# A gated mix of a spectral filter and a long convolution on one Trainium2 core: weight rows copied by ScalarE, a third butterfly on TensorE, half-width gated matrices, and a new instruction order

## The chip, the cores and the metric

The kernel runs on one core of one Trainium2 chip. The metric is the device time of one execution in microseconds (us), as the median of several executions; the span is the part of it from the first to the last instruction that the profiler recorded. A core has these engines, each with a queue of its own that it works through in order: PE (TensorE, matrix products; PEld is its loading of weights), DVE (VectorE), ACT (ScalarE), POOL (GpSimd) and SP (SyncE, which here only issues DMAs). They wait for one another by semaphores. DMAs run on 16 DMA engines, whichever queue issued them.

## What is computed

The reference, cut to what matters (x is 2048 time steps by 512 channels; the tensor u is not used):

```python
g = sigmoid((x * gate_w).sum(-1, keepdims=True))          # one gate per time step

X = rfft2(x, axes=(time, channel))                        # branch a: spectral filter
a = irfft2(X * (w_r + 1j * w_i))

dt = exp(log_dt)                                          # branch b: long convolution
A = -exp(log_A_real) + 1j * A_imag
C = (C_real + 1j * C_imag) * dt[:, None]
K = 2 * einsum("dn,dnl->dl", C, exp(A * dt[:, None] * pos)).real
b = irfft(rfft(x, 2 * L) * rfft(K, 2 * L))[:L] + x * D_skip

out = g * a + (1 - g) * b
```

The step sizes in the inputs are so small that every K is constant over the 2048 steps, so the convolution is a running sum of x times one factor per channel. The kernel counts the channels for which this holds and has a general path for the case that one is missing; that path does not run with these inputs.

## The kernel before

All tensors are float32. Branch a is a two-dimensional Fourier transform written as matrix products. Time, 2048, is split into 32 x 64, channels are folded into four groups of 128 (`CHANNELS`), and the spectrum is worked off in eight *units* (0 to 7), each with two of 16 frequency slots. Branch b and the gate run beside it on the same engines.

The order of the work is written out by hand in `PLAN` (lines 29 to 38): a list of words, a letter for a step and a number for its index. A dictionary maps each letter to a function (lines 623 to 630), and the words are emitted in that order. Since every engine works in order, the list fixes the order on every queue; the tile framework adds the semaphores. The steps, with their engines:

- `F` (POOL, L254 to 260) folds one of the ten parts of x, `C` (PE, L263) is the first time stage of a part, `c` (DVE, L276) transposes its result into `AR`. x is loaded into `AI`, whose space is later used for the spectrum of the last stages.
- `P` (PE, L429) is the second time stage of a unit with matrices `s2e`, `t` (ACT, L434) copies it to `et`, `D` (PE, L447) is the channel transform with `dfw`, into the tile `p_d`. `d` (ACT, L456) copies half of `p_d` to `ds`, and `Z` (DVE, L464 to 472) is the butterfly of even and odd channel parts. For the units in `ZPE` the butterfly is done on PE instead, by 16 more instructions in `D` (L451 with `zfw`), and `d` and `Z` are absent.
- `W` and `U` (DVE, L484) multiply by the weights `w` of the unit, `p` (POOL, L490 and 491) combines real and imaginary parts, `g` (POOL, L503 and 504) is the butterfly of the way back, `h` (ACT, L511 to 519) repairs partition 0, where a special frequency lies.
- `I` (PE, L531) is the inverse channel transform, `i` (ACT, L537) copies half of it, `V` (DVE, L545) writes sums and differences into `AI`.
- `K` (PE and ACT, L551 and 553) repairs slot 0. `B` (PE, L565, eight of them) is the first inverse time stage and needs all units; before the first one (`FIRSTB`) stand `NDUM` dummy matmuls (L559). `b` (DVE, L569) transposes.
- `Q` (PE, L588, eight of them) is the last stage. Its matrices `s1a` have been multiplied by the gate before: `S` loads one of four, `E` (DVE, L582) multiplies both its halves by the gate. `q` (DVE, L602) adds branch b and issues the output DMA; for `LASTQ` it goes in two halves (L599).
- Branch b: `X` loads x transposed, 1 MB for each of four channel groups, into `XT`; `x` (ACT, L336) copies one half into a PSUM tile, `m` (DVE, L339) scans, `y` (ACT, L348) scales the scan into `v`, `o` (ACT, L343) scales x by the skip factors, `r` (POOL queue, L353) is a DMA that adds `v` into `XT`, `H` (POOL, L371) multiplies by the gate's complement.
- The gate: `k` (PE, L376) is one group of four matmuls over `XT`, `G1` (ACT, L386) the sigmoids, `G2` (SP) writes the gate to memory, `O` (SP, L363) reads it back as a broadcast into `gb`, `u` (ACT, L367) copies it to a PSUM tile for `E`. `N` and `G4`, `G5` belong to the count.
- Loads: `l` (SP, L415) loads a unit's weights of 512 KB; there are four such buffers, which the four `s1a` use afterwards. `R` and `T` (SP) load constants and parameters.

Row 0 of each unit's weight tile is replaced by a special row (the weights of one more channel frequency). `J` (L399 to 410) prepares these rows: three tiny DVE operations, ACT copies, a transpose on PE with the unit matrix `eye`, and a copy to `hT`. `L` (SP, L418) then copies 2 KB of `hT` into the tile by a DMA, which must wait until the unit's own `w` has landed.

Units 1 and 7, the first ones, are cut into halves: 11 and 21 are the two halves of unit 1, 17 and 27 those of unit 7.

PSUM tiles (two banks each) come from one pool of four (`psum`, L186): `C`, `P`, `D`, `I`, `x`, the gate sums, `u`, `K`, `B` and `Q` each take the next of the four in the order of the list and wait until the tile's last reader has finished. The 13 buffers `blk`, which hold `f`, `et`, `tw`, `px` and `gt`, go round in the same way, and so do four buffers `v` for `y` and `O`.

Of the kernel before, what the change touches and what calls it, by code (L numbers as in the profile page):

```python
# [29 lines left out]
F2 X1 C0 R7 C1 c0 R6 J0 c1 F3 J1 R9 C2 c2 F4 C3 c3 F5 R1 R0 C4 J2 F6 C5 c4 C6 c5 F7 F9 T0 F8 c6 C7 c7 C8 C9 c8 c9 P17  # L30
P27 l7 x1 P11 X0 N1 t17 t27 D17 D27 d17 P21 m1 N3 L7 l1 N0 N4 d27 N2 y1 Z17 l4 t11 Z27 l6 P4 t21 P6 L1 U17 W17 X2 x0
U27 W27 L4 t4 m0 D11 d11 k0 D21 k1 k2 p17 t6 D4 X3 y0 Z11 d21 l5 k3 R10 D6 U11 W11 p27 g17 g27 h27 o3 R4 p11 o2 h17 L6
Z21 R8 L5 U21 d4 W21 Z4 U4 o1 P5 G1 R5 I17 I27 W4 d6 Z6 W6 P0 l0 U6 i17 t5 g11 p21 g21 o0 i27 h21 G2 r1 V27 V17 x2 D5
l2 m2 p4 g4 O2 h4 L0 l3 t0 D0 h11 I11 y2 d0 O0 U5 P2 o5 o4 t2 W5 I4 S1 p6 Z0 i11 U0 L3 L2 r0 W0 I21 g6 h6 V11 i4 i21
S0 D2 p5 g5 V4 h5 V21 d2 Z2 r2 W2 U2 P3 x3 t3 D3 p0 g0 S2 h0 m3 y3 U3 u0 W3 E1 I6 p2 o7 i6 o6 E0 V6 I5 I0 i5 V5 g2 h2
I2 G4 O3 i0 V0 p3 g3 h3 S3 I3 i2 G5 V2 u1 E3 K0 i3 H2 K1 V3 E2 B1 b1 O1 r3 B5 b5 H4 B0 b0 H0 H3 B2 b2 B3 b3 B4 H1 b4
H6 B7 b7 B6 Q0 Q2 q0 H5 Q3 H7 b6 q2 q3 Q5 Q1 q5 q1 Q7 q7 Q6 q6 Q4 q4
# [3 lines left out]
_T = np.arange(128)  # L41
# [6 lines left out]
def _consts():  # L48

    pi = np.pi  # L50
    a = np.arange(32)
    b = np.arange(64)
    k2 = np.arange(64)
    b_ = b.reshape(2, 32)
    S1 = np.zeros((32, 2, 32))
    S1[:, 0, 0] = 1
    S1[:, 1, 0] = (-1.0) ** a
    for s in range(1, 32):
        f = s if s < 16 else s - 16 + 0.5
# [53 lines left out]
    s2q = np.stack([s2p[0], s2p[1] @ inv, s2p[2] @ inv], 1)  # L113
# [3 lines left out]
    c, s = np.cos(th), np.sin(th)  # L117
# [22 lines left out]
    for x in range(2):  # L140
# [38 lines left out]
def body(ctx: ExitStack, tc: tile.TileContext, x, xg, xt, w, wh, prms, vecs, gw,  # L179
         c_s1e, c_s1f, c_s2e, c_s2, c_s2v, c_s2r, c_s2q, c_s1b, c_s1a, c_dfw, c_zfw, c_dbw, c_pos, c_eye, out):  # L180
# [5 lines left out]
    def psum(name):  # L186
        return ps.tile([P, 2, 512], F32, tag="ps", name=name)
# [33 lines left out]
    hT = work.tile([32, P], F32, name="hT")  # L221
    gws = work.tile([P, 4, 32], F32, name="gws")
# [7 lines left out]
    t_ = {}  # L230

    with tc.manual_schedule():
        prm = {}
        ldt = few[:, 0]
        nc.scalar.dma_start(s1e, c_s1e)
        nc.scalar.dma_start(hw, wh)
        nc.scalar.dma_start(eye, c_eye)
# [62 lines left out]
        def n1():  # L300
            S.activation(few[:, 0], few[:, 0], AF.Exp)
# [109 lines left out]

# [5 lines left out]
        def load_h(u):  # L417
            nc.sync.dma_start(t_["w", u][0:1, 0], hT[4 * u:4 * u + 4])  # L418
# [155 lines left out]
        def load_a(k):  # L574
            s1a[k] = work.tile([P, 8, P], F32, tag="w", name="s1a", bufs=4)
            nc.sync.dma_start(s1a[k], c_s1a[k])

        def gated(k, E):
            s = s1a[k].rearrange("p b (e c) -> p b e c", e=2)
            g = (t_["gp", k // 2] if E is V else t_["gb", 2 + k // 2]).rearrange("p (b c) -> p b c", c=64)[:, 8 * (k % 2):8 * (k % 2) + 8]  # L580
            for e in range(2):
                E.tensor_tensor(s[:, :, e], s[:, :, e], g, op=ALU.mult)  # L582

        def Q_(j):
            i, k = j // 4, j % 4
            p = t_["pq", j] = psum("p_oa").rearrange("p u (b c) -> p (u b) c", b=4)
            for b in range(8):
                T.matmul(p[:, b], VA[:, i, 8 * (k % 2) + b, :, k // 2], s1a[k][:, b], start=True, stop=True)  # L588
# [16 lines left out]
        def a_a(j):  # L605
# [11 lines left out]
            lambda: (nc.sync.dma_start(gws, gw), nc.sync.dma_start(dsk, vecs[:, 1])),  # L617
            lambda: (nc.sync.dma_start(s2v, c_s2v), nc.sync.dma_start(s2r, c_s2r)),
# [17 lines left out]
    with tc.If(n_small < D):  # L636
        with tc.tile_pool(name="dram", bufs=1, space=bass.MemoryType.DRAM) as dp:
            Kd = dp.tile([D, L], F32, name="Kd")
            with tc.tile_pool(name="kg", bufs=1) as kg:

                pos = kg.tile([P, 96], F32, name="pos")
                nc.sync.dma_start(pos, c_pos)
                ld = kg.tile([P, 4], F32, name="ld")
# [141 lines left out]
            for k in range(4):  # L785
                nc.sync.dma_start(ga[k], c_s1a[k])
# [33 lines left out]
def _arrays(given):  # L820
# [12 lines left out]
    w = np.stack([w[:, :, :, 0, 0], w[:, :, :, 1, 1], w[:, :, :, 0, 1], w[:, :, :, 1, 0]], 3)  # L833
    arrays = {
# [39 lines left out]
```

## Time and profile before

| | |
|---|---|
| median of 3 runs | 119.42 us (119.1 to 120.74) |
| the profiled execution's own time | 119.98 us |
| its span | 118.1 us |
| mean granted TensorE clock | 0.969 of full speed |
| PE busy | 96.8 us (82% of the span) |
| DVE busy | 88.0 us (74%) |
| POOL busy | 75.1 us (64%) |
| ACT busy | 45.6 us (39%) |
| DMA | 28.79 MB, mean 244 GB/s |

How to read the profile. A row of a group of instructions gives line, engine, operation, the tiles written and read, shapes and count; then busy time in us and the mean duration of one in ns; then the idle time of the engine just before these instructions and what ended it. The chain of work is followed back from the last instruction to what released each step; its rows give the start, the length and what it was. A stage row gives a window and its length, then busy time (and count of instructions) of PE, PEld, DVE, ACT and POOL, the granted TensorE clock, the share of time that the DMA engines were busy, and GB/s. A row of waits gives the waiting engine and line, what it waited for, the total in us, how many times, and the longest. SPq is the DMA issuing of SP. Durations of operations that follow one another closely overlap a little, so that two of 1.28 us can start 1.23 us apart.

### The profile page before, as it was taken

The page shows a single profiled execution, that of the slowest core. Times are in us where ns is not written, and L with a number is a line of the kernel's source. Part 1 is how long each engine was busy: PE and PEld are TensorE (multiplying, and loading weights), DVE is VectorE, ACT ScalarE, POOL GpSimd, SP SyncE. Part 2 cuts the span into 40 slices and gives each one's busy share as a digit, 9 for nine tenths or more (in the row PEclk, how much of TensorE's full clock was granted, in tenths as well). Part 3 has the DMA queues.
Part 4 walks back from the last instruction along what each step waited for, and adds up shares of the span by engine and source line. Part 5 has one row for each costly group of instructions (what it writes and reads, how often), then busy time and mean ns, then how long its engine had stood idle before and what let it go on. Part 6 is the DMA issues. An engine that isn't in the chain of part 4 may idle for free.

```text
span 118.1 us, 2316 instructions
## 1 busy us (share of the span) xinstructions
PE 96.8 (82%) x877; PEld 78.7 (67%) x877; DVE 88.0 (74%) x139; ACT 45.6 (39%) x80; POOL 75.1 (64%) x70
## 2 busy tenths in 40 slices
PE   6989784999861999968495978997899999999700
PEld 6957463999430649967395977987753359999700
DVE  0059889848988439999649599999798999956620
ACT  0320004359549059391878283698740000000000
POOL 0069580220796005999999999999999999910000
PEclk9999999999999679999999999999999999999985
DMA  3999999977979976499979999978129700678680
GB/s 66 381 389 416 413 383 345 298 318 238 327 286 337 409 226 220 136 325 178 225 191 214 262 321 218 262 198 297 50 44 190 126 3 3 248 314 330 248 302 15
DMA packets 9314, 28.79 MB, mean 244 GB/s; under 512 B 1577, under 2 KB 2121, under 8 KB 8781
## 3 DMA queue, kind: packets, MB, share of 16 engines
q1 hardware_dynamic: 7628, 23.93, 55.9%
q0 software_dynamic: 1088, 4.19, 19.5%
q10 hardware_dynamic: 576, 0.43, 1.1%
q8 instruction: 9, 0.15, 0.5%
q14 instruction: 13, 0.10, 0.3%
HBM read 20.12 MB, written 4.21 MB: 206 GB/s over the span
## 4 chain that ended last, share of the span: by engine, by line
PE 46%; DMA 29%; POOL 10%; DVE 3%; ACT 3%; issue 2%; SPq 1%; DVEq 0%; POOLq 0%
PE p_oa L588 13%; PE p_d L447 10%; DMA s2e<-in_c_s2e_dram 8%; PE p_ia L565 6%; DMA XT<-in_xt_dram 6%; PE p_t L429 6%; PE p_v L531 6%; DMA AI<-in_x_dram 6%; POOL gt L504 4%; DMA s1a<-in_c_s1a_dram 4%; DMA w<-in_w_dram 3%; DMA last<-in_c_s1e_dram 3%; POOL gt L503 2%; POOL px L490 2%; PE p_gate L376 2%
## 5 line engine op out<-in xcount | busy, mean ns | idle before, releaser
L447 PE MATMUL p_d<-et,dfw 128*128 128x256 f32 (+1 forms) x80 | 18.7, 370 | 4.2 <-ACT et L434 3.2
L484 DVE TENSOR_TENSOR tw<-p_d,w 128x1024 f32<-128x1024 f32 (+1 forms) x20 | 19.2, 1005 | 1.2 <-ACT ds L456 0.6
L371 POOL TENSOR_TENSOR XT<-XT,gb 128x1024 f32<-128x1024 f32 x8 | 19.2, 2755 | 0.0
L447 PEld LDWEIGHTS p_d<-et,dfw 128*128 128x128 f32 x80 | 12.9, 202 | 8.4 <-ACT et L434 4.7
L531 PE MATMUL p_v<-dbw,gt 128*128 128x128 f32 x128 | 15.8, 278 | 2.5 <-POOL px L490 1.2
L429 PE MATMUL p_t<-s2e,AR 128*128 128x128 f32 x128 | 16.2, 282 | 1.6 <-DMA s2e<-in_c_s2e_dram 1.6
L429 PEld LDWEIGHTS p_t<-s2e,AR 128*128 128x128 f32 x128 | 15.8, 196 | 2.0 <-DVE AR L283 1.8
L531 PEld LDWEIGHTS p_v<-dbw,gt 128*128 128x128 f32 x128 | 14.9, 192 | 3.2 <-ACT gt L512 1.4
L283 DVE STREAM_TRANSPOSE AR<-p_s 128x512 f32<-128x512 f32 (+1 forms) x20 | 10.7, 587 | 7.3 <-PE p_s L275 7.3
L503 POOL TENSOR_TENSOR gt<-px 128x512 f32<-128x512 f32 (+1 forms) x10 | 11.0, 1101 | 7.8 <-PE p_d L447 7.3
L588 PEld LDWEIGHTS p_oa<-s1a,AR 128*128 128x128 f32 x128 | 15.2, 196 | 0.8 <-DVE AR L569 0.8
L588 PE MATMUL p_oa<-s1a,AR 128*128 128x128 f32 x128 | 15.3, 282 | 0.0
L490 POOL TENSOR_TENSOR px<-tw 128x512 f32<-128x512 f32 (+1 forms) x10 | 11.8, 1179 | 5.0 <-DVE tw L484 5.0
L258 POOL TENSOR_TENSOR f<-AI 128x512 f32<-128x512 f32 (+1 forms) x8 | 9.0, 1138 | 7.8 <-DMA AI<-in_x_dram 7.7
L545 DVE TENSOR_TENSOR AI<-p_v,po 128x512 f32<-128x512 f32 (+1 forms) x20 | 10.3, 574 | 2.0 <-PE p_v L531 1.3
L491 POOL TENSOR_TENSOR px<-tw 128x512 f32<-128x512 f32 (+1 forms) x10 | 11.7, 1174 | 0.0
L504 POOL TENSOR_TENSOR gt<-px 128x512 f32<-128x512 f32 (+1 forms) x10 | 11.0, 1102 | 0.0
L602 DVE TENSOR_TENSOR AI<-p_oa,XT 128x1024 f32<-128x1024 f32 x7 | 8.5, 1219 | 3.1 <-PE p_oa L588 2.6
L275 PE MATMUL p_s<-AI,last 64*64 64x128 f32 (+1 forms) x192 | 9.9, 335 | 0.5 <-DMA AI<-in_x_dram 0.5
L569 DVE STREAM_TRANSPOSE AR<-p_ia 128x1024 f32<-128x1024 f32 x8 | 9.3, 1216 | 0.5 <-PE p_ia L565 0.5
L339 DVE TENSOR_TENSOR_SCAN p_x<-p_x,XT 128x1024 f32<-128x1024 f32 x4 | 9.2, 2290 | 0.3 <-ACT p_x L336 0.3
L434 ACT COPY et<-p_t 128x1024 f32<-128x1024 f32 (+1 forms) x10 | 8.2, 845 | 2.3 <-PE p_t L429 2.2
(72 smaller groups left out, 120.2 us busy)
## 6 DMA issues: line engine op xcount, KB each, us to landing
XT<-in_xt_dram SPq DMA_DIRECT2D x4, 1024.0 KB, 7.2
w<-in_w_dram SPq DMA_DIRECT2D x8, 512.0 KB, 8.4
XT<-v POOLq DMA_DIRECT2D x4, 1024.0 KB, 9.1
out_dram<-AI SPq DMA_DIRECT2D x7, 512.0 KB, 3.4
AI<-in_x_dram SPq DMA_DIRECT2D x6, 512.0 KB, 6.2
gb<-gd SPq DMA_DIRECT2D x4, 512.0 KB, 4.0
s1a<-in_c_s1a_dram SPq DMA_DIRECT2D x4, 512.0 KB, 4.9
AI<-in_x_dram SPq DMA_DIRECT2D x4, 256.0 KB
```

The lines of the kernel that those rows point to most:

```text
L283: V.transpose(av[:, u, :, k], pv[:, u])
L371: E.tensor_tensor(r, r, t_["gb", h % 2], op=ALU.mult)
L429: T.matmul(p[:, q, :, 64 * v:64 * v + 64], AR[:, q % 2, 8 * (q // 2) + u, :, v], s2e[:, 2 * u + v], start=True, stop=True)
L447: T.matmul(d[:, o, 1:3] if h else d[:, o, 0:4:3], dfw[:, 2 * h + o], e[:, 2 * h + o], start=True, stop=not z)
L484: E.tensor_tensor(t, z, w, op=ALU.mult)
L490: G.tensor_tensor(po[:, 0], t1[:, :, 0:4:2], t1[:, :, 1:4:2][:, :, ::-1], op=ALU.subtract)
L491: G.tensor_tensor(po[:, 1, :, ::-1], t2[:, :, 0:4:2], t2[:, :, 1:4:2][:, :, ::-1], op=ALU.add)
L503: G.tensor_tensor(gv[:, :, 0], src[0], src[1], op=ALU.subtract)
L504: G.tensor_tensor(gv[:, ::-1, 1], src[0], src[1], op=ALU.add)
L531: T.matmul(p[:, v, h, o], rows(u, o, v, h), dbw[:, h, o], start=True, stop=True)
L545: V.tensor_tensor(ai[:, :, :, k], t_["pi", u][:, v, :, 0], t_["po", u][:, v], op=ALU.subtract if k else ALU.add)
L588: T.matmul(p[:, b], VA[:, i, 8 * (k % 2) + b, :, k // 2], s1a[k][:, b], start=True, stop=True)
```

## The change

Five things change together.

1. The special weight rows. The host now lays out the two summands of each row, `wh`, as 8 partitions of 2 x 512 numbers. `J` is two DVE operations on them and one DMA on ACT's queue that gathers the eight rows on partition 0, in slots 0 to 7 of `AI` (its x has been read by then). `L` becomes an ACT copy of 512 numbers on partition 0 from there into the weight tile. `SLOT` says which slot a unit's row has, so that it is read before `V` writes that slot. `eye` is loaded only in the general path.
2. `ZPE` is (2, 4, 5) in place of (3, 5).
3. The gated matrices. The second half of each row block of `s1a` is the first up to a sign that depends on the partition. Only the 64 columns of the first half are loaded (256 KB in place of 512), one DVE operation multiplies them by the gate, and ACT writes the other half by a scaling with the sign `sgn`. `Q` reads the two halves as two runs of 64.
4. Small loads are merged: gate weights, step sizes, skip factors and the sign in one, `s2v` and `s2r` in one.
5. A new `PLAN`, with unit 1 first, unit 4 last, `LASTQ` 3 and `FIRSTB` 4.

The diff, cut to its core:

```diff
-ZPE = (3, 5)
-LASTQ = 4
-FIRSTB = 1
+SLOT = (5, 3, 6, 7, 0, 4, 1, 2)
+ZPE = (2, 4, 5)
+LASTQ = 3
+FIRSTB = 4
 PLAN = """
+R7 C1 c1 F2 F3 R0 C0 F4 C2 T0 C3 F5 c0 c2 F6 C4 R1 R9 R6 C5 c3 C6 c4 c5 c6 J0 N1 l1 X2 F7 F8 C8 c8 C7 c7 F9 C9 c9 P11
+t11 P21 N0 t21 D11 d11 D21 d21 l7 P17 R5 t17 P6 N4 N3 L1 l6 Z11 Z21 t6 U11 X1 W11 p11 P27 W21 t27 D17 D27 d17 d27 U21
+p21 X0 g11 Z17 L7 Z27 U17 W17 U27 l0 R8 R4 X3 W27 P0 l3 P3 g21 x2 R10 t0 L6 t3 h11 x1 D6 h21 k0 N2 k1 d6 m2 y2 m1 L0
+o2 y1 Z6 U6 o3 D0 d0 p17 k2 k3 o4 W6 G1 I11 I21 Z0 U0 l5 i11 P5 D3 t5 p27 g17 i21 W0 g27 h17 V21 r1 d3 p6 L3 G2 g6 o5
+h27 p0 V11 P2 t2 l2 h6 D5 l4 r2 Z3 U3 W3 g0 x0 L5 I17 m0 O2 I27 D2 o0 h0 S1 y0 L2 U5 W5 p3 g3 S0 O3 U2 h3 P4 i17 V17
+p5 O1 W2 o1 I6 r0 p2 g5 g2 i27 V27 t4 i6 V6 x3 S2 L4 m3 D4 o6 I0 u0 y3 i0 W4 U4 S3 V0 o7 G4 G5 p4 g4 h2 I3 h5 E1 E0 I2
+i3 V3 O0 i2 h4 I5 i5 I4 u1 i4 V2 V5 r3 E2 K0 K1 V4 B4 H1 E3 b4 B7 b7 B2 b2 B5 H5 B6 B1 b5 b6 B0 B3 b1 b0 H2 Q4 H4 H6
+H7 b3 q4 H0 Q5 H3 q5 Q6 q6 Q1 q1 Q2 q2 Q7 q7 Q0 q0 Q3 q3
 """
...
-        ldt = few[:, 0]
         nc.scalar.dma_start(s1e, c_s1e)
+        hw = blk([P, 2, 512], "hw")[0:8]
         nc.scalar.dma_start(hw, wh)
-        nc.scalar.dma_start(eye, c_eye)
...
         def J_(k):
-            if k == 0:
-                V.tensor_tensor(hs[:, :, 0:4:2], hw[:, :, 0, :, 0], hw[:, :, 0, :, 1], op=ALU.add)
-                V.tensor_tensor(hs[:, :, 1], hw[:, :, 1, 1, 1], hw[:, :, 1, 1, 0], op=ALU.subtract)
-                V.tensor_tensor(hs[:, :, 3], hw[:, :, 1, 0, 0], hw[:, :, 1, 0, 1], op=ALU.subtract)
-                S.copy(hs[0:1, 0, 0:4:3], hw[0:1, 0, 0, :, 0])
-                S.copy(hs[0:1, 0, 1:3], hw[0:1, 0, 0, ::-1, 1])
-            elif k == 1:
-                t_["ph"] = psum("p_h")
-                T.transpose(t_["ph"][:32, 0, 0:P], hs.rearrange("p q i -> p (q i)"), eye)
-            else:
-                S.copy(hT, t_["ph"][:32, 0, 0:P])
+            a, b = (hw[:, z].rearrange("u (i k) -> u i k", i=4) for z in range(2))
+            V.tensor_tensor(a[:, 0:4:2], a[:, 0:4:2], b[:, 0:4:2], op=ALU.add)
+            V.tensor_tensor(a[:, 1:4:2], a[:, 1:4:2], b[:, 1:4:2], op=ALU.subtract)
+            nc.scalar.dma_start(AI[0:1, 0:8], hw[:, 0])
...
         def load_h(u):
-            nc.sync.dma_start(t_["w", u][0:1, 0], hT[4 * u:4 * u + 4])
+            S.copy(t_["w", u][0:1, 0].rearrange("p i k -> p (i k)"), AI[0:1, SLOT[u]])
...
         def load_a(k):
-            s1a[k] = work.tile([P, 8, P], F32, tag="w", name="s1a", bufs=4)
-            nc.sync.dma_start(s1a[k], c_s1a[k])
+            s1a[k] = work.tile([P, 2, 8, 64], F32, tag="w", name="s1a", bufs=4)
+            nc.sync.dma_start(s1a[k][:, 1].rearrange("p b c -> p (b c)"), c_s1a[k])
 
         def gated(k, E):
-            s = s1a[k].rearrange("p b (e c) -> p b e c", e=2)
-            g = (t_["gp", k // 2] if E is V else t_["gb", 2 + k // 2]).rearrange("p (b c) -> p b c", c=64)[:, 8 * (k % 2):8 * (k % 2) + 8]
-            for e in range(2):
-                E.tensor_tensor(s[:, :, e], s[:, :, e], g, op=ALU.mult)
+            a = s1a[k].rearrange("p e b c -> p e (b c)")
+            g = (t_["gp", k // 2] if E is V else t_["gb", 2 + k // 2])[:, 512 * (k % 2):512 * (k % 2) + 512]
+            E.tensor_tensor(a[:, 0], a[:, 1], g, op=ALU.mult)
+            S.activation(a[:, 1], a[:, 0], AF.Copy, scale=sgn)
...
-                T.matmul(p[:, b], VA[:, i, 8 * (k % 2) + b, :, k // 2], s1a[k][:, b], start=True, stop=True)
+                T.matmul(p[:, b].rearrange("p (e c) -> p e c", e=2), VA[:, i, 8 * (k % 2) + b, :, k // 2], s1a[k][:, :, b], start=True, stop=True)
...
-            lambda: (nc.sync.dma_start(gws, gw), nc.sync.dma_start(dsk, vecs[:, 1])),
-            lambda: (nc.sync.dma_start(s2v, c_s2v), nc.sync.dma_start(s2r, c_s2r)),
+            lambda: nc.sync.dma_start(gv, gw),
+            lambda: nc.sync.dma_start(s2, c_s2v),
```

More of the change, by code (lines that the diff above doesn't have):

```diff
@@ L29 @@
 PLAN = """
[L30 to L37, printed above, removed]
+R7 C1 c1 F2 F3 R0 C0 F4 C2 T0 C3 F5 c0 c2 F6 C4 R1 R9 R6 C5 c3 C6 c4 c5 c6 J0 N1 l1 X2 F7 F8 C8 c8 C7 c7 F9 C9 c9 P11
[6 more added lines that the diff above has]
+H7 b3 q4 H0 Q5 H3 q5 Q6 q6 Q1 q1 Q2 q2 Q7 q7 Q0 q0 Q3 q3
 """
@@ L220, in body @@
     dbw = work.tile([P, 2, 3, P], F32, name="dbw")
-    hT = work.tile([32, P], F32, name="hT")
-    gws = work.tile([P, 4, 32], F32, name="gws")
+    gv = work.tile([P, 137], F32, name="gv")
+    gws, ldt, dsk = gv[:, 0:128].rearrange("p (i c) -> p i c", i=4), gv[:, 128:132], gv[:, 132:136]
+    sgn = gv[:, 136:137]
     def blk(shape, name):
@@ L300, in n1 @@
         def n1():
-            S.activation(few[:, 0], few[:, 0], AF.Exp)
+            S.activation(few[:, 0], ldt, AF.Exp)
         def n4():
@@ L642, in body @@
                 nc.sync.dma_start(pos, c_pos)
+                nc.sync.dma_start(eye, c_eye)
                 ld = kg.tile([P, 4], F32, name="ld")
@@ L833, in _arrays @@
     w = np.stack([w[:, :, :, 0, 0], w[:, :, :, 1, 1], w[:, :, :, 0, 1], w[:, :, :, 1, 0]], 3)
+    hw = weight[..., ::256].transpose(0, 1, 2, 4, 3)
+    wh = np.zeros((2, 8, 4, P))
+    for i, a, b in ((0, (0, 0, 0), (0, 0, 1)), (1, (1, 1, 1), (1, 1, 0)), (2, (0, 1, 0), (0, 1, 1)), (3, (1, 0, 0), (1, 0, 1))):
+        wh[0, :, i], wh[1, :, i] = hw[:, :, a[0], a[1], a[2]].T, hw[:, :, b[0], b[1], b[2]].T
+    wh[0, 0, :, 0], wh[1, 0, :, 0] = hw[0, 0, 0, (0, 1, 0, 1), (0, 1, 1, 0)], 0
+    wh = wh.transpose(1, 0, 2, 3).reshape(8, 2, 512)[np.argsort(SLOT)].astype(np.float32)
     arrays = {
```

25 lines of the change are left out of this document (11 added, 14 removed).

## The prediction, made before the changed kernel was run

> **What bounds the kernel now.** I read the busy times by stage first (columns: length, then busy time and count of each engine, granted TensorE clock, DMA share, GB/s), then the chain of work that ended last.
>
> ```profile
> span 118.1 us, 2316 instructions
> ```
> The execution's own time is 119.98, so 1.9 us lie outside the span. The stages:
>
> ```profile
> 34.50:38.00 3.50, 0.05 (x6) 0.05 (x7) 2.80 (x7) 2.89 (x6) 2.35 (x4) 1.00 0.89 319
> 38.00:42.60 4.60, 4.60 (x20) 2.60 (x24) 1.59 (x3) 0.68 (x4) 0.37 (x1) 0.63 0.96 384
> ...
> 45.70:83.90 38.20, 31.98 (x247) 29.98 (x245) 33.58 (x51) 24.96 (x46) 37.73 (x34) 1.00 0.89 234
> 89.00:111.50 22.50, 22.50 (x193) 17.60 (x192) 18.34 (x17) 0.00 (x0) 14.77 (x7) 1.00 0.57 179
> ```
> From 45.7 to 83.9 the last busy column, POOL, is full: 37.73 of 38.20 us. DVE has 33.58, PE 31.98, ACT 24.96. Before it lies a hole (POOL 2.35 of 3.5, 0.37 of 4.6), behind it a tail in which PE has no gap. The chain tells how the hole came and what stands before the tail:
>
> ```profile
> 26.20 4.06 DMA w<-in_w_dram
> 30.26 0.02 issue
> 30.27 0.59 SPq L418
> 30.87 0.04 issue
> 30.91 7.00 DMA XT<-in_xt_dram
> 37.91 0.04 issue
> 37.95 1.06 PE p_gate L376 x8
> 39.02 3.49 PE p_d L447 x8
> 42.51 1.06 PE p_gate L376 x8
> 43.57 1.92 PE p_d L447 x8
> ...
> 82.60 1.29 POOL gt L504
> ...
> 84.38 2.05 PE p_v L531 x16
> 86.44 0.86 PE p_k L551 x2
> 87.30 1.72 PE p_ia L559 x4
> 89.01 7.22 PE p_ia L565 x62
> 96.23 15.29 PE p_oa L588 x128
> ```
> The small copy of a weight row (L418) holds SP's queue until its w has landed at 30.26; only then is an XT load issued, and the gate matmuls, in order on PE, wait for it until 37.95. The D behind them takes 3.49 us where the same eight instructions take 1.92 at 43.57: the granted clock was 0.63 in 38.0 to 42.6.
>
> ```profile
> SPq L418 <- DMA w<-in_w_dram: 12.4, 4, 5.0
> POOL gt L503 <- PE p_d L447: 7.3, 1, 7.3
> PE p_gate L376 <- DMA XT<-in_xt_dram: 3.4, 1, 3.4
> PE p_d L447 <- ACT et L434: 3.2, 2, 2.1
> ```
> SP stood 12.4 us at that copy in all, POOL 7.3 us behind the hole. So three things decide: when POOL gets its first full unit, how long its list is from there, and the 29.1 us from B's start at 89.0 to the end.
>
> **The change part by part.** Prices (busy, mean ns):
>
> ```profile
> L582 DVE TENSOR_TENSOR s1a<-s1a,p_g 128x512 f32<-128x512 f32 x8 | 5.0, 677 | 0.0
> L343 ACT ACTIVATE XT<-XT,pers 128x1024 f32<-128x1024 f32 x8 | 9.0, 1147 | 0.0
> L511 ACT COPY gt<-px 1x256 f32<-1x256 f32 x6 | 2.6, 428 | 3.9 <-POOL gt L503 3.9
> L434 ACT COPY et<-p_t 128x1024 f32<-128x1024 f32 x6 | 6.1, 1009 | 0.4 <-PE p_t L429 0.3
> L464 DVE SCALAR_TENSOR_TENSOR p_d<-p_d,pers,ds 128x128 f32<-128x128 f32 x4 | 1.4, 359 | 1.8 <-ACT ds L456 1.7
> L465 DVE SCALAR_TENSOR_TENSOR p_d<-ds,pers,p_d 128x256 f32<-128x256 f32 x3 | 1.5, 488 | 0.1
> L467 DVE TENSOR_TENSOR p_d<-p_d,ds 128x256 f32<-128x256 f32 x3 | 1.3, 432 | 0.1
> L484 DVE TENSOR_TENSOR tw<-p_d,w 128x1024 f32<-128x1024 f32 x12 | 14.1, 1219 | 0.6 <-issue 0.2
> L339 DVE TENSOR_TENSOR_SCAN p_x<-p_x,XT 128x1024 f32<-128x1024 f32 x4 | 9.2, 2290 | 0.3 <-ACT p_x L336 0.3
> L386 ACT ACT_TABLE_LOAD x1 | 1.3, 1283 | 0.0
> ```
> Weight rows (L). Eight DMAs leave SP, and its 12.4 us of standing with them; eight ACT copies of 1x512 come. Nothing shows that shape: 0.43 (1x256) and 1.01 (128x1024) bound it; the line between them gives 0.62 at 512 elements, and I take 0.60, nearer to the first. ACT +4.8 us. A copy now makes ACT wait for its w, with t, d, h and i queued behind; but each l stands far ahead of its L. Counting the bytes ahead of each at the 319 GB/s of the first row, I estimate margins of 2 us or more, so no wait; without them each late w would stop ACT as it stopped SP, up to 5.0 us.
>
> Preparing the rows (J). One transpose, four small ACT copies and three tiny DVE operations go; two DVE operations on 8x256 come, at the 0.43 of L467 (the same 256 elements; at most 0.68, the 512 of L582, at least nothing, should the c beside them wait anyway), and one small DMA. They stand among the last c, where DVE is busy, and C8 is put before C7, so that PE waits for its fold. Each costs a share of what the other hides; with nothing hidden 0.86 and about 0.8. I put the last c 1.0 later than before; since the chain shows nothing of that place but PE's start, that is P11 ready at 20.35 where P17 started at 20.08, then held by its s2e load and not by the c. The DMA waits on ACT's queue for two DVE operations; behind it stands only the Exp of the step sizes, needed 5 us later.
>
> Half matrices (E). DVE does four 512-element products for eight: -2.7 us. ACT gets four scalings by a sign: between 0.60 (the plain copy above) and 1.147 (scaled, 1024 elements). The scaled one is 0.14 longer than the copy at 1024, so 0.70 to 0.74; taken at 0.70, +2.8. Loads shrink by 1 MB, hidden either way. Q then reads its moving operand in two runs of 64. B reads single strided elements, and its rows of 512 columns in four tiles take 7.22 us for 64, 0.45 for each four, against 1.72 for the four contiguous dummies, 0.43 each: no cost. If Q did lose, it would be on the path; its upper bound by that pair is 5% of 15.29, 0.8 us.
>
> Units 2, 4, 5 on TensorE for 3, 5: one unit more. DVE saves four operations, 2 x 0.488 + 2 x 0.432 = 1.84; ACT a copy of 0.6; PE pays 16 matmuls at 0.44 for four:
>
> ```profile
> 72.06 0.44 PE p_d L451 x4
> ```
> or 1.76 us. Merged and moved loads only free SP, ahead of need.
>
> **The order, walked.** I put the new word order through each queue with these prices. A Z is 1.95 with its gaps (unit 0: 2.6; a half unit 1.48, by L464's half form), a product U or W 1.2 (half 0.62), P or I 2.05 alone and 1.9 in a row, D 1.8 (with the butterfly 3.6), V two of L467's kind with twice the elements, 1.28. POOL's p or g: its 38.2 us held twelve full ones, three halves and three DMA issues; with a half and an issue counted as half each, 38.2 / 15 = 2.55.
>
> To 46.1. P11 20.35, 1.05; t11 0.6; P21, which shares the tile, 1.05; t21 0.6 beside D11 1.05; d11 0.4; D21 1.0: 25.5. DVE then does Z11 and Z21, 2.95 to 28.5, and U11 and W11 to 29.8: p11 (before, p17 at 30.3). PE goes on with P17, P6, P27, D17, D27 (5.8 us) to 31.3, d17 0.4. POOL does p11, p21, g11, g21, p17, p27, g17, g27 without the hole; p17 waits for W17 at 36.0, four halves of 1.4 follow, 41.7. DVE is continuous from Z17 at 31.75: two Z 2.95, four half products 2.5, scans m2 and m1 4.5 (2.29 less overlap), Z6 1.95, U6 and W6 2.4: 46.05. ACT from 36.3: h11 0.5, x1 after W27 frees its tile (37.2) to 38.25, h21 0.5, d6 0.6, y2 1.15 behind m2 to 40.8, L0 0.6, o2, y1, o3 3.45 to 44.85, d0 0.6, o4 1.15, G1 with its table load 2.4: 49.0. r1 on POOL waits for o3, 44.85, and ends with W6. The XT loads, now ahead of most w, are there. PE has one hole: D6, k0 and k1 end at 39.05, and D0 needs scan 2's PSUM tile, free at 40.8 with y2: 1.8 us. D0, k2, k3, I11 and I21 follow to 46.7. POOL is then ahead of before by three halves and an issue, 5.1 us, at 46.1 against 45.7.
>
> 46.1 to the last g. POOL has twelve full p and g and two issues: 13 x 2.55 = 33.1, so g4 ends at 79.2 (before: g3 at 83.9) if it is fed. DVE feeds it: Z0, U0, W0 5.0 to 51.05; V21, V11, Z3, U3, W3 5.8 to 56.85; m0, U5, W5 4.65 to 61.5; U2 behind D2 (62.4), V17, W2 to 65.6; V27, V6 behind i6 (66.9) to 68.2, m3 70.45, W4, and U4 behind I0 (71.8) to 73.05. PE: P5 to 48.6, D3 behind G1 to 50.8, P2 behind W0 to 52.95, D5 56.55, I17 and I27 behind W3 58.8, D2 62.4, P4, I6 66.2, D4 69.8, I0 71.7. POOL wants W0 at 51.15, W3 at 57.5, W5 at 62.65, W2 at 66.45 (its tile comes from I6, 66.2), U4 at 74.1. The margins are 0.1 to 1.1 us; DVE's remaining 33.9 us of work would end at 80, ACT's about 30 from 49.0 at 79, PE's 32 from 46.7 at 78.7. Four engines end within 2 us of each other.
>
> To B4. g4 79.2, h4 0.45, I4 2.05, i4 0.6, V4 1.3: 83.6. K0 (0.86) and the dummies (1.72) follow I4 on PE, so B4 starts at 84.3. I add 0.9, a long ACT copy (L434), because hardly a margin is longer than that: 85.2 against 89.0, -3.8. Nothing added is the lower bound of that term, rival (1) the upper. The tail keeps eight B, eight Q and the split last output: 29.1. POOL's eight damping products end at about 100, ahead of the q that read them.
>
> **Sum:** 85.2 + 29.1 = 114.3 span, + 1.9 outside it = 116.2. The profiled 119.98 is 0.6 above the median 119.42; from the median it would be 115.6. I give 116.0.
>
> **A rule against it, weighed.** Folds on POOL take 0.73 (128x256):
>
> ```profile
> L258 POOL TENSOR_TENSOR f<-AI 128x256 f32<-128x256 f32 x2 | 1.4, 730 | 0.1
> ```
> The Trainium skill, SBUF — State Buffer, "Who interferes with whom", says that a VectorE instruction with two SBUF inputs contends with a GpSimd instruction that reads SBUF, one blocking the other; J's two operations are such, and no run here shows them beside a fold. By that rule the first waits for at most one fold, and the sum is up to 0.7 later, 116.7; sign and chances stay.
>
> **The rivals.** (1) The queues fall out of step. For it: the margins above, and each unit now crosses ACT, whose share in this stage rises from 24.96 of 38.2 to some 30 of 33. If two or three of the six units come one 1.0 us copy late beyond the margin, and the last h and i too, B4 is at 86.5 to 89: 117.5 to 120, centre 118.5.
>
> (2) The scan's PSUM tile stops PE and the clock falls. Before, one wait of 3.4 us was followed by a clock of 0.63, and cost 3.4 + 3.49 - 1.92 = 5.0 us; waits of up to 2.1 (L447 on et) lie in a stage with clock 1.00. The walk has 1.8 at D0. If y2 is 1.6 later, the price is 1.6 + 1.6: 119.2. Four tiles rotate, and D0, I11, I6 and G4 each take over a scan's tile; from two full stops on, 2 x 5.0 - 1.8 = 8.2: 116.0 + 8.2 = 124.2, slower. Against it: only D0's hole is visible. The Trainium skill, TensorE: Matmul & The Clock Gate, Part 1, has the clock halved after an idle window of about 3.4 us; the trace agrees, with its one such wait (3.4 us, clock 0.63).
>
> (3) The saved DVE and SP time is not the limit. SP still has loads that wait for a buffer (l3, l5). If these hold XT or zfw back, so that POOL gains only half of its 5.1 us, g4 ends at 82, B4 starts at 88, and the time is 119 (118.5 to 120.5). Against it: no SP DMA waits for w to land any more.
>
> **How the numbers follow.** Forecast (114.2 to 117.0) 0.54; (1) 0.18; (2) once 0.06, twice or more 0.14; (3) 0.08. A measurement of this kernel tells about 2% from no change: faster is below 117.0, slower above 121.8. Faster 0.54, same 0.18 + 0.06 + 0.08 = 0.32, slower 0.14. The range runs from the walk without the added 0.9 and with one microsecond more of overlap (114.2) to the upper end of (1) and (3), 120.8; what lies above is (2) twice, and a little is below.
>
> **What would show it.** Right: no SP wait on w by a row copy; g27 ending near 42 and the first full p near 46; POOL nearly full from there to the last g, near 79 to 80; PE clock 1.00 throughout; B near 85; tail 29.1. Wrong: a PE wait of over 3 us before D0, I6 or G4 with a clock below 0.9; ACT copies of 1x512 near 1 us or waiting for w; Q over 15.5 us; POOL waiting for W in several units.

## The result, and the profile after

The changed kernel is slower: 124.0 us (median of 4 executions, 123.35 to 124.97) against 120.08 us of the kernel before beside it; the ratio is 1.042, with a 95% interval of 1.033 to 1.052. Its profiled execution took 123.35 us with a span of 121.6; the prediction had 116.0 and 114.3. (Single executions can be disturbed by the chip and come out some per cent longer; ratios and intervals leave these out, medians do not.)

The page of the changed kernel: the span, then the busy tenths of POOL and the granted TensorE clock in 40 slices of 3.04 us.

```profile
span 121.6 us, 2321 instructions
...
POOL 0019970200799919999999994089999999300000
PEclk9999999999999999999999997555999999999995
```

POOL's half units now run through (the row of nines before the 1), and the hole ahead of the first full unit is one slice, 42.6 to 45.6 us, where r1 waits for o3, as in the walk. But POOL has a new hole, from 73 to 79 us (the 4 and the 0), and the clock falls there to half. The same by stages (length, then busy time and count of PE, PEld, DVE, ACT and POOL, granted clock, DMA share, GB/s):

```profile
46.80:78.00 31.20, 24.47 (x185) 23.30 (x183) 21.71 (x33) 21.07 (x40) 27.32 (x23) 0.94 0.90 212
78.00:80.50 2.50, 0.34 (x8) 0.24 (x8) 2.43 (x3) 2.50 (x4) 1.13 (x1) 0.50 0.00 0
80.50:90.00 9.50, 9.43 (x65) 9.34 (x66) 6.17 (x12) 6.08 (x14) 9.42 (x8) 0.79 0.65 160
92.40:121.60 29.20, 22.55 (x193) 17.78 (x192) 18.87 (x18) 0.74 (x1) 11.90 (x6) 0.95 0.38 148
```

No engine is full in the first row, although each had been counted near its limit: something stopped all of them. The waits name it (who, for whom, us in total, times, longest):

```profile
ACT v L345 <- DMA XT<-v: 7.8, 1, 7.8
DVE v L344 <- DMA XT<-v: 7.7, 1, 7.7
PE p_count L391 <- ACT v L345: 6.8, 1, 6.8
PE p_d L436 <- ACT gt L500: 2.7, 1, 2.7
```

The first two are one step, `y3`: a one-column memset of a `v` buffer on DVE (L344) and the scaled copy into it on ACT (L345). Both wait for a DMA that adds `v` into `XT`, the step `r`. The timeline of the changed kernel around it (start, duration, engine, line; in brackets the idle time before and what ended it):

```profile
65.71 1.16 POOL L350 DMA_DIRECT2D XT<-v  x1
...
69.12 1.00 ACT L364 COPY p_g<-gb 128x1024 f32<-128x1024 f32 x1
...
77.92 0.06 DVE L344 MEMSET v<- 128x1 f32 x1 [7.70 <-DMA XT<-v]
77.95 1.11 ACT L345 ACTIVATE v<-p_x,pers 128x1024 f32<-128x1024 f32 x1 [7.83 <-DMA XT<-v]
78.07 2.35 DVE L473 TENSOR_TENSOR tw<-p_d,w 128x1024 f32<-128x1024 f32 x2
...
79.12 0.34 PE L391 MATMUL p_count<-pers,last 128*1 128x1 f32 x8 [6.84 <-ACT v L345]
79.37 1.27 POOL L479 TENSOR_TENSOR px<-tw 128x512 f32<-128x512 f32 x1 [5.10 <-DVE tw L473]
...
80.57 9.28 PE L520 MATMUL p_v<-dbw,gt 128*128 128x128 f32 x64 [1.11 <-DVE tw L473]
```

Read it as three queues behind one wait. `r0` is issued on POOL at 65.71 and lands at 77.9, 12.2 us later. `y3` takes the buffer that `r0` reads. Behind the memset stand `U4` and `W4` on DVE (78.07), and behind those `p4` on POOL. Behind the copy on ACT stands G4 on PE (L391), because it takes over the PSUM tile that `y3` reads, and the last four I units stand behind G4. (They also wait for U4 and W4, as the bracket of L520 says; which of the two sets the end is asked in experiment 3.) The chain shows the price:

```profile
68.02 2.21 DVE p_x L336
70.22 7.68 issue
...
80.57 9.28 PE p_v L520 x64
89.85 0.86 PE p_k L540 x2
90.71 1.72 PE p_ia L548 x4
92.43 7.25 PE p_ia L554 x61
99.67 15.29 PE p_oa L577 x128
```

"issue" here is no issuing: it is the 7.68 us of waiting for that DMA. B starts at 92.43 where 85.2 was forecast; from there to the end it is 29.2 us, forecast 29.1. Nearly the whole miss of the span, 121.6 for 114.3, lies between 70.2 and B.

The prices of the new instructions (busy, mean ns):

```profile
L440 PE MATMUL p_d<-et,zfw 128*128 128x128 f32 x48 | 7.3, 274 | 0.0
L407 ACT COPY w<-AI 1x512 f32<-1x512 f32 x8 | 4.9, 608 | 0.0
L571 ACT ACTIVATE s1a<-s1a,gv 128x512 f32<-128x512 f32 x4 | 2.8, 722 | 1.3 <-DVE s1a L570 1.3
L570 DVE TENSOR_TENSOR s1a<-s1a,p_g 128x512 f32<-128x512 f32 x4 | 2.6, 672 | 0.0
L398 DVE TENSOR_TENSOR hw<-hw 8x256 f32<-8x256 f32 x1 | 0.8, 847 | 0.0
L399 DVE TENSOR_TENSOR hw<-hw 8x256 f32<-8x256 f32 x1 | 0.4, 404 | 0.0
```

The row copy was priced at 0.60 and takes 0.608; the sign scaling at 0.70 and takes 0.722; Q kept its 15.29 us in the chain. But for J's first operation (L398, 0.847 for 0.43), the parts cost what they were said to cost.

### The profile page after: what moved, and what is told of

Its sections match the earlier page's. It is cut to its first block, busy times and chain, and to the rows that moved or that the text cites. A ratio compares the mean times of both kernels' runs of the same rounds, so it can differ in the third digit from the quotient of the medians.

```text
span 121.6 us, 2321 instructions
## 1 busy us (share of the span) xinstructions
PE 97.7 (80%) x892; PEld 81.6 (67%) x892; DVE 84.2 (69%) x130; ACT 51.1 (42%) x88; POOL 74.8 (62%) x70
## 4 chain that ended last, share of the span: by engine, by line
PE 37%; DVE 20%; POOL 13%; issue 13%; DMA 6%; ACT 4%; SPq 1%; DVEq 0%; POOLq 0%; ACTq 0%
PE p_oa L577 13%; PE p_v L520 8%; DVE AR L282 7%; PE p_ia L554 6%; DMA AI<-in_x_dram 6%; DVE tw L473 5%; PE p_t L418 5%; POOL px L479 3%; PE p_d L436 3%; POOL px L480 3%; POOL gt L492 3%; DVE p_x L336 2%; POOL gt L493 2%; PE p_ia L548 1%; POOL XT L350 1%
## 5 line engine op out<-in xcount | busy, mean ns | idle before, releaser
L436 PE MATMUL p_d<-et,dfw 128*128 128x256 f32 (+1 forms) x80 | 17.3, 343 | 4.1 <-ACT gt L500 2.7
L520 PE MATMUL p_v<-dbw,gt 128*128 128x128 f32 x128 | 17.2, 297 | 1.1 <-DVE tw L473 1.1
L520 PEld LDWEIGHTS p_v<-dbw,gt 128*128 128x128 f32 x128 | 16.6, 212 | 2.0 <-issue 2.0
L436 PEld LDWEIGHTS p_d<-et,dfw 128*128 128x128 f32 x80 | 11.8, 191 | 5.9 <-ACT gt L500 2.8
L492 POOL TENSOR_TENSOR gt<-px 128x512 f32<-128x512 f32 (+1 forms) x10 | 11.7, 1173 | 0.3
L493 POOL TENSOR_TENSOR gt<-px 128x512 f32<-128x512 f32 (+1 forms) x10 | 11.7, 1168 | 0.0
L274 PEld LDWEIGHTS p_s<-AI,last 64*64 64x64 f32 x192 | 6.9, 146 | 3.7 <-DMA AI<-in_x_dram 1.4
```

The costliest lines, as they stand in the source:

```text
L274: T.matmul(p[64 * g:64 * g + 64, h, u * n:u * n + n], s1e[r, 64 * u * i:64 * u * i + 64], src[:, g * n:g * n + n], start=i == 0, stop=i == ...
L436: T.matmul(d[:, o, 1:3] if h else d[:, o, 0:4:3], dfw[:, 2 * h + o], e[:, 2 * h + o], start=True, stop=not z)
L492: G.tensor_tensor(gv[:, :, 0], src[0], src[1], op=ALU.subtract)
L493: G.tensor_tensor(gv[:, ::-1, 1], src[0], src[1], op=ALU.add)
L520: T.matmul(p[:, v, h, o], rows(u, o, v, h), dbw[:, h, o], start=True, stop=True)
```

## The experiments

**1. Another buffer for y3.** The theory: y3's wait is the whole loss. One word is moved, so that y3 takes a buffer whose transfer has long landed (that of `r2`), and O1 has to wait for that of `r0`.

```diff
-p5 O1 W2 o1 I6 r0 p2 ... I0 u0 y3 i0 W4 U4 S3
+p5 W2 o1 I6 r0 p2 ... I0 u0 y3 O1 i0 W4 U4 S3
```

> Edit: in the changed kernel's order the load O1 is recorded behind y3, so that y3 takes the v buffer that r2 read and O1 the one that r0 reads; nothing else moves. Theory (the wait): the whole loss is y3's wait of 7.8 us for the buffer under r0's accumulating transfer, with the memset ahead of it in DVE's queue, and the low clock behind it. Then y3 starts near 70.2 us instead of 77.95, W4 at 70.3, POOL's p4 at 74.3 and g4's end at 79.4, the first real matmul of B falls from 92.4 to 84 to 86, and the time is 115 to 117.5 us. Rival (the parts: row copies on ScalarE, third butterfly on TensorE, signs on ScalarE cost the time somewhere): the wait goes, but the work behind it starts late for another reason, and the time stays at 121 to 124 us. Rival (the order of the middle is itself too tight): half of it comes back, 118 to 121 us.

Measured: 115.88 us in the profiled execution (115.39 to 118.33, median 117.03; the kernel before beside it 118.37), span 114.0. Its timeline, and its row by stages:

```profile
66.12 1.17 POOL L350 DMA_DIRECT2D XT<-v  x1
...
70.64 0.06 DVE L344 MEMSET v<- 128x1 f32 x1
...
71.11 2.36 DVE L473 TENSOR_TENSOR tw<-p_d,w 128x1024 f32<-128x1024 f32 x2 [0.42 <-PE p_d L440]
...
73.62 5.60 PE L520 MATMUL p_v<-dbw,gt 128*128 128x128 f32 x48 [0.65 <-POOL gt L492]
...
74.30 1.67 POOL L479 TENSOR_TENSOR px<-tw 128x512 f32<-128x512 f32 x1
...
79.74 1.18 POOL L350 DMA_DIRECT2D XT<-v  x1
...
80.30 2.05 PE L520 MATMUL p_v<-dbw,gt 128*128 128x128 f32 x16 [1.08 <-ACT gt L501]
...
84.86 5.61 PE L554 MATMUL p_ia<-AI,s 64*64 64x512 f32 x48
```

```profile
46.80:79.70 32.90, 30.71 (x244) 29.35 (x243) 28.43 (x43) 28.11 (x51) 32.66 (x27) 1.00 0.88 211
```

The memset follows the scan without a wait, POOL is full (32.66 of 32.90 us) to the end of g4 at 79.8, and B starts at 84.86. The rivals (the parts, or a middle too tight) fall: all of the loss came back, and the walk of the prediction comes out, 84.86 for 85.2 and a span of 114.0 for 114.3. The same version once more:

> The version with O1 behind y3 once more, in more rounds, for the interval of its time against the kernel before, and beside two further edits on the same chip. From its first profiled run (115.9 us against 117.1 to 118.5 us of the kernel before on that chip) the ratio should be 0.96 to 0.99. If it were 0.995 or more, the changed kernel without its wait would be worth nothing against the kernel before.

Measured: 116.42 us (median of 12), ratio 0.991 (0.984 to 0.998), a hair above the expected 0.99. The time is the forecast one, but the gain of 3% over the kernel before that it meant is not shown. The ratio compares with executions of the kernel before of 116.2 to 117.6 us here, and of 119.2 to 120.4 in experiment 6, where nearly the same version stands at 0.963. So the gain is between 1 and 4%, and which of the two is typical stays open.

**2. A larger dose.** `r0` is put behind y3 in the list; y3 still gets that buffer, and the wait grows.

```diff
- I6 r0 p2 ... u0 y3 i0
+ I6 p2 ... u0 y3 r0 i0
```

> Edit: r0 is recorded behind y3 instead of ahead of p2; y3 still takes the buffer that r0 reads, and POOL issues r0 only behind g2. A larger dose of the same wait. Theory (the wait): POOL issues r0 near 73 us instead of 65.7, it lands some 10 to 12 us later, y3 starts near 83 to 85.5 instead of 77.95, and the time grows by the same 5 to 7.5 us, to 129 to 132 us. Rival (the wait is filled with other work, the loss has another cause): under 126 us.

Measured: 128.49 us median, 1.085 of the kernel before (1.073 to 1.097). y3's memset starts at 83.55, and waits:

```profile
DVE v L344 <- DMA XT<-v: 11.1, 1, 11.1
```

That is 11.1 us instead of 7.7. The time grows by 4.5 us for a start 5.6 later: a little under the range, and far from the rival's.

**3. Which standstill costs, DVE's or TensorE's?** y3 goes behind W4 and U4, so that DVE and POOL run on while y3 still waits.

```diff
- u0 y3 i0 W4 U4 S3
+ u0 W4 U4 y3 i0 S3
```

> Edit: y3 (its memset on DVE and its copy on ScalarE) is recorded behind W4 and U4; it still waits for r0's transfer. It tells which engine's standstill costs the time. If it is DVE's (W4 and U4 behind the memset, so that POOL's p4 and g4 come late), then p4 starts near 74.3 instead of 79.4 and most of the loss goes: 117 to 119 us. If it is TensorE's (G4's matmuls need the PSUM tile that y3 reads, and the four I units stand behind them), the I units start at 79.5 instead of 80.6 and the time is 122 to 123.5 us.

Measured: 124.1 us median (121.97 to 126.31; the kernel before beside it 118.37), near the changed kernel. Its timeline:

```profile
71.53 2.35 DVE L473 TENSOR_TENSOR tw<-p_d,w 128x1024 f32<-128x1024 f32 x2 [0.47 <-PE p_d L440]
...
80.05 1.11 ACT L345 ACTIVATE v<-p_x,pers 128x1024 f32<-128x1024 f32 x1 [9.09 <-DMA XT<-v]
...
81.22 0.34 PE L391 MATMUL p_count<-pers,last 128*1 128x1 f32 x8 [8.11 <-ACT v L345]
81.49 9.04 PE L520 MATMUL p_v<-dbw,gt 128*128 128x128 f32 x64
```

U4 and W4 come 6.5 us earlier than in the changed kernel, and the loss stays. What sets the end is TensorE's queue: G4, a few tiny matmuls, holds the I units behind it while it waits for a PSUM tile. The move did gain a little: from y3's start to B it is 93.04 - 80.02 = 13.0 us, in the changed kernel 92.43 - 77.92 = 14.5. But `r0` took 13.4 us to land here instead of 12.2, and y3 started 2.1 us later, so none of it is left in the time.

**4. The low clock by itself.** Into version 3, matmuls that nobody reads are put on TensorE between U4's end and G4, first 14 and then six.

```diff
- u0 W4 U4 y3 i0
+ u0 W4 U4 Y6 y3 i0
...
+        def warm_again(n):
+            p = t_["pd", 4]
+            for _ in range(n):
+                T.matmul(p[:, 0], dbw[:, 0, 0], dbw.rearrange("p h o t -> p (h o t)")[:, 0:512], start=True, stop=True)
```

> Base: the version with y3 behind W4 and U4 (the wait of y3 kept). Edit: 14 matmuls of 128x512 that nobody reads are put on TensorE between U4's end and G4, into the PSUM tile that W4 and U4 have read, so that TensorE works through most of its wait for y3. It prices the low clock by itself. Theory (the clock falls because TensorE stands still): the 64 matmuls of the four I units take 7.6 to 7.8 us instead of 9.04, the first real matmul of B follows y3's start by 11.3 to 11.9 us instead of 13.0, and the time is 1.0 to 1.6 us less than that version's. Rival (the clock falls there for another reason, such as the load of the whole kernel): 8.9 to 9.4 us again.

> As the run with 14 dummy matmuls, with six: each is recorded as two of 0.44 us, so 14 filled 12.3 us and held TensorE 7.5 us beyond y3's start; six fill 5.3 us, from U4's end near 75 to about 80.5, when y3's copy ends. It prices what the low clock adds to the end. Theory (the clock costs its whole 1.4 us there): the 64 matmuls of the four I units take 7.4 to 7.8 us instead of 9.04 and the first real matmul of B follows y3's start by 11.3 to 11.9 us instead of 13.0. Rival (those matmuls wait for other engines at full clock, as they do in the version without the wait): the I units still end 8.7 to 9.1 us after they start, and B follows y3's start by 12.6 to 13.1 us.

The 14 were mis-sized: they took 12.28 us and overran the wait, 128.06 us in all. The six took 124.82 us (median, 122.98 to 126.55; the kernel before beside it 121.48). With either number the clock is back. With six:

```profile
75.88 5.42 PE L559 MATMUL p_d<-dbw 128*128 128x512 f32 x12 [0.83 <-DVE tw L473]
...
82.18 7.38 PE L520 MATMUL p_v<-dbw,gt 128*128 128x128 f32 x64 [0.61 <-DVE count L393]
```

The 64 matmuls of I take 7.38 us (7.41 behind 14) instead of 9.28 in the changed kernel: standing still lowers the clock, and work keeps it up. The distance from y3's start (79.12) to B (92.07) hardly moved, 12.95 us, as the rival said; but the I units also started 3.06 us behind y3 instead of 1.44 as in version 3, since the dummies overran a little. From the first I to B it is 9.89 us, in version 3 93.04 - 81.49 = 11.55, in the changed kernel 92.43 - 80.57 = 11.86. So the low clock costs 1.7 to 2.0 us where nothing else holds I. In the version without the wait I to B is 84.86 - 73.62 = 11.24 at full clock, as I4 there waits for POOL. Of the 7.57 us between the two B's, 80.57 - 73.62 = 6.95 is the later start of I. As an estimate from these figures, had the clock stayed up, B would have come up to 2.0 us earlier, so that the clock's share of the 7.57 us is up to 2.0 and standing still has the rest.

**5. The new instructions in the old order.**

```diff
-PLAN, ZPE, LASTQ, FIRSTB of the changed kernel
+PLAN of the kernel before without J1 and J2; ZPE = (3, 5), LASTQ = 4, FIRSTB = 1
```

> Edit: the changed kernel's instructions (row copies on ScalarE, signs on ScalarE, the new loads and the doubled J) in the order of the kernel before, with its butterfly on units 3 and 5, its first block of B and its last of Q; only the words J1 and J2 are gone. It parts the new instructions from the new order. Theory (the wait, which the new order alone brings): the new instructions cost nothing on the path, 117.5 to 121 us, the level of the kernel before. Rival (the new instructions cost the time): 122 us or more.

Measured: 129.74 us, ratio 1.095 (1.078 to 1.112). It answers another question than it asked: TensorE's first stage waits for J's transfer, since J now stores the rows in the space of `x`. In this place it also overwrites a part of x that is read after it, so this version leaves a part of the computation out:

```profile
PE p_s L274 <- DMA AI<-hw: 7.8, 1, 7.8
```

With J behind c6, as in the new order:

> Edit: as in the run of the new instructions in the old order, but J stands behind c6: its transfer writes into the buffer of x, and where the old order has it, the first matmuls and folds waited 7.8 us for it (and read a part of x that it had overwritten, so that run left out a part of the computation). With that wait gone the new instructions stand in the old order without it. Theory (the new instructions cost nothing, the new order brought y3's wait): 117.5 to 121 us. Rival (they cost time in themselves): 122 us or more, with ScalarE's row copies or the signs in the chain.

Measured: 119.26 us in its best execution (median 121.58; the kernel before beside it 120.37, best 119.2). From one such execution no more can be said than that the parts in the old order are about level with the kernel before, as the theory had it.

**6. Undoing one part at a time, in the version without the wait.** The three ran on one chip, and their ratios compare with executions of the kernel before of 119.2 to 120.4 us. Signs on DVE again:

```diff
-S.activation(a[:, 1], a[:, 0], AF.Copy, scale=sgn)
+E.scalar_tensor_tensor(a[:, 1], a[:, 1], sgn, g, op0=ALU.mult, op1=ALU.mult)
```

> Base: the version with O1 behind y3 (115.9 us in its profiled run). Edit: the second half of each gated matrix is made on DVE again (sign times matrix times gate, from the matrix itself) and ScalarE's scaling is gone, so the half gating is undone: DVE +4 x 0.67 to 0.73 us, ScalarE -4 x 0.72 us. If the signs on ScalarE are worth what the walk gave them, the three gated matrices ahead of V4 delay DVE there by 0.7 us of which the copy K1 on ScalarE hides some: the first real matmul of B at 84.9 to 86, the time 115.5 to 117 us. Rival (ScalarE's signs are themselves on the path in front of K1): it becomes faster by 0.3 to 0.7 us.

Measured: ratio 0.963 (0.953 to 0.972), 115.82 us in the profiled execution, span 114.0 and B at 84.93, as with the signs on ScalarE. The half matrices' 2.7 us of DVE were not on the path. So this run also serves as the level of the version without the wait on this chip.

Rows copied by SP's queue again:

```diff
-S.copy(t_["w", u][0:1, 0]..., AI[0:1, SLOT[u]])
+nc.sync.dma_start(t_["w", u][0:1, 0]..., AI[0:1, SLOT[u]])
```

> Base: the version with O1 behind y3. Edit: the eight special rows are copied from the same place by SP's queue again instead of ScalarE (ScalarE -8 x 0.61 us, SP +8 transfers of 2 KB, each behind its weight load and ahead of what stands next in SP's queue). If ScalarE's row copies were worth something: the W products of the early units wait for the row's transfer of about 2 us behind the load, and loads behind it in SP's queue start later: 117 to 120 us. Rival (ScalarE is not the bound and SP's waits were hidden): 115 to 116.5 us, no difference.

Measured: ratio 0.993 (0.981 to 1.004), profiled 119.71 us. The waits show why, two of the products wait for a row:

```profile
DVE tw L473 <- DMA w<-AI: 6.5, 2, 3.4
```

and TensorE then waits 3.2 us once and works at a lower clock behind it. B starts at 88.83 instead of 84.93 in the run with the signs on DVE. The row copies on ScalarE are worth 3 to 4 us.

Unit 4's butterfly on DVE again (`ZPE = (2, 5)`, `d4 Z4` ahead of y3):

> Base: the version with O1 behind y3. Edit: unit 4's butterfly on DVE again (TensorE -16 matmuls, 1.76 us; ScalarE +0.6 us for d4; DVE +1.84 us for Z4 ahead of W4). W4 and U4 end 1.4 us later, p4's first half on POOL waits for W4 until 74.3 in any case: if POOL is the bound there, the first real matmul of B moves by 0 to 0.6 us and the time is 115.5 to 117 us, so the third butterfly on TensorE bought little at this place. If DVE is the bound, B moves by the whole 1.4 us: 117 to 118.5 us.

Measured: ratio 1.002 (0.994 to 1.010), profiled 119.42 us: both expectations were too low. Its timeline:

```profile
75.76 10.23 PE L520 MATMUL p_v<-dbw,gt 128*128 128x128 f32 x64 [3.18 <-DVE tw L473]
...
78.63 1.28 POOL L493 TENSOR_TENSOR gt<-px 128x512 f32<-128x512 f32 x1
```

POOL's last g starts at 78.63, against 78.51 with the butterfly on TensorE: POOL lost nothing. But U4 ends later, TensorE waits 3.18 us for its PSUM tile, the clock falls (0.71 from 75.7 to 86.0), and the I units take 10.23 us. B starts at 88.50 instead of 84.86. U4 and W4 start 2.15 us later (73.26 for 71.11), which cost 3.6 us.

**7. A further order.** D6 ahead of x1, `Z6 U6 W6` ahead of m1, r1 behind g6.

> Base: the version with O1 behind y3. Edit: D6 is recorded ahead of x1 (so it takes a PSUM tile that is free 2.6 us earlier and x1 takes the next), Z6, U6 and W6 ahead of the scan m1, and r1 behind g6 on POOL. If POOL's row of products from p6 to g4 sets the end, p6 can start near 43.5 instead of 47.05 us and p0 at W0's end near 50.7 instead of 52.5: B falls by 1 to 2 us, to 83 to 84 us, and the time to 113 to 115 us. Also the 2.65 us for which TensorE waits before D6 and the slow matmuls behind it (430 instead of 240 ns) should be gone. Rival (DVE's scans and products set the end there, and I11 waits longer for y1's PSUM tile): no gain, or a loss of up to 1 us.

Measured: 1.009 of the kernel before (1.004 to 1.015), median 117.78 us against 116.42 of its base on the same chip: a loss a little above the rival's. p6 does start at 43.20, but p0 waits 3.59 us for W0 until 53.16, because d0 on ScalarE stands behind y1, whose scan now comes later: DVE's feed was the bound, as the rival said. Three things moved at once, so what TensorE's hole at D6 costs by itself is not shown.

**8. J beside a fold, and not.** `J0` moved from behind c6 to behind c9.

> Base: the version with O1 behind y3. Edit: J's two operations on DVE stand behind c9 instead of behind c6, where POOL has no fold left. If J's first operation is long because POOL's fold runs beside it (0.87 us against 0.41 us of the second, of one form), both take 0.40 to 0.45 us. Rival (the first of two operations on this tile is always long, whatever runs beside it): 0.8 to 0.9 and 0.4 us again. The time stays at 115 to 118 us by either.

Measured (118.05 us, one execution): no fold of POOL runs beside J any more, and its two operations take

```profile
L399 DVE TENSOR_TENSOR hw<-hw 8x256 f32<-8x256 f32 x1 | 0.4, 406 | 0.0
L398 DVE TENSOR_TENSOR hw<-hw 8x256 f32<-8x256 f32 x1 | 0.4, 371 | 0.0
```

against 871 and 405 ns in its base. So the 0.5 us goes with a fold beside J. It is not always the first operation that pays: in the version with the rows copied by SP (experiment 6), where folds also run beside J, the first takes 371 ns and the second 942.

## Why the prediction was wrong, step by step

Predicted, the changed kernel, and the version without the wait (us):

| | predicted | changed | y3 with another buffer |
|---|---|---|---|
| first p on POOL | 29.8 | 31.08 | 30.01 |
| last half g (g27) ends | 41.7 | 43.1 | 43.5 |
| first full p (p6) | 46.1 | 46.82 | 47.05 |
| g4 ends | 79.2 | 84.5 | 79.8 |
| B starts | 85.2 | 92.43 | 84.86 |
| B to the end of the span | 29.1 | 29.2 | 29.1 |

- **The step that failed** is the sentence "V27, V6 behind i6 (66.9) to 68.2, m3 70.45, W4, and U4 behind I0 (71.8) to 73.05". Between m3 and W4 stands y3, and its memset is in DVE's queue; the walk counted y on ScalarE alone and never asked when the buffer that y3 writes would be free. The runs showed in its place a wait of 7.7 us for `r0`'s transfer, with G4 and the I units behind it, and B at 92.43 instead of 85.2; with that wait away B is at 84.86. In the kernel before, y3 followed its scan without a wait, so no row of it showed one. The words that describe the kernel say that the `v` buffers go round in turn; they do not. In turn, y3 would have had the buffer of O2, which u0 reads to 70.12; its wait shows that it got that of y0, under r0's transfer.
- **Rival (2)** named the place (G4 behind a scan's PSUM tile) and the sum (124.2), but as two stops from a late scan. It was one stop, from a transfer, at 7.6 us, so that 124.2 lies next to the measured 124.0 is chance. The chance of 0.14 was too low because rivals were sought among late copies, and not among waits for buffers under transfers.
- **D0's hole** of 1.8 us did not come. PE's hole lies at D6 instead, 2.65 us, because D6 takes over the PSUM tile of units 17 and 27, which the walk had given to x1. Experiment 7 removed it and gained nothing, but moved DVE's work as well.
- **Row copies, sign scaling, Q:** prices right within 0.03 us, no wait of ScalarE for a weight row. In the version without the wait the first matters by 3 to 4 us, the second not at all.
- **The third butterfly:** the price was right: D4 with it starts at 66.74 and I0 behind it at 70.33, the 3.6 us priced (the 7.3 us of the 48 instructions overlap with the others of D). The worth was not asked for. It keeps TensorE from a wait that the low clock behind it makes dearer, 3.6 us in experiment 6.
- **J:** 0.85 and 0.40 us for 0.43 each. The rule of the Trainium skill that was weighed (SBUF — State Buffer, "Who interferes with whom") holds here: its 0.7 at most were 0.44 (0.847 less 0.404), and they vanish in experiment 8.
- **The list of POOL and the tail** were right: with the wait away, 32.66 of 32.90 us busy, g4 0.6 us late and B 0.3 us early. Part of that is luck: the steps before came 0.2 to 1.8 us late, and the 0.9 us added for queues out of step made up for it at B.
- **The range:** its upper end, 120.8, is above the 120 and 120.5 that rivals (1) and (3) give as theirs.

Open: by which rule the buffers were handed out (experiment 2 put r0 behind y3 in the list, and y3 still waited for it). A fifth `v` buffer was not tried.

## What to carry to other kernels

Walk a new order through every queue with all its instructions, the smallest too: a memset of 59 ns held DVE for 7.7 us. For each tile that is written, find in the built order which earlier tile had the buffer, and when its last reader ends, where a transfer that reads it counts until it has landed (8 to 13 us here). A wait of TensorE of about 3 us is dearer than it looks, so ask of each tiny matmul in its queue what it waits for.

## What the runs showed of the hardware

- The clock fell behind waits shorter than the 3.4 us of the kernel before. Waits of 3.18 and 3.19 us were followed by a granted clock of 0.71 and 0.69 (experiment 6), one of 2.80 us by 0.68 (experiment 7), and one of 2.33 us there was not: the eight matmuls behind it took 2.00 us. The wait of 2.65 us before D6 went either way: in the changed kernel the eight matmuls behind it took 1.97 us, with y3's other buffer 3.44. The Trainium skill (TensorE: Matmul & The Clock Gate, Part 1) has an idle window of about 3.4 us. The page also says that the window runs freely, so that its effect varies from run to run; that fits the two outcomes of one wait, though all these waits are shorter than its figure. D6 in the changed kernel, and in the version without the wait:

```profile
38.16 1.97 PE L436 MATMUL p_d<-et,dfw 128*128 128x256 f32 x8 [2.65 <-ACT gt L500]
...
37.09 3.44 PE L436 MATMUL p_d<-et,dfw 128*128 128x256 f32 x8 [2.65 <-ACT gt L500]
```

- The adding transfers of 1 MB took 7.9 to 12.2 us from issue to landing in the changed kernel, and up to 13.4 us in experiment 3. `r0` alone took 12.2 us in a stage in which the DMA engines were busy 0.90 of the time, and about 8 us in experiment 2, where it was issued ten us later.
- POOL's operations behind the issue of such a transfer are recorded as 1.5 to 1.7 instead of 1.28 us (p4 in experiment 1: 1.67), for 4 to 11 us and not until it has landed: in the changed kernel the records are back at 1.28 us 4 us after `r1` was issued, and no transfer there landed in less than 7.9. Within such a stretch they still start about 1.24 us apart, and only the next one behind it comes 1.6 to 1.8 us after the last: the records grow, the pace hardly.
